# The second layer's first weights made by spaced steps in the last first-layer entry; last carried output evicted before the late work

## Chip, cores and metric

The kernel runs on one core of a Trainium2 chip. The metric is the device time of one execution in microseconds (us), median of three runs; lower is better. A profiled execution gives, beside its own time, a trace of every instruction on the engines: PE (matrix engine, with its weight loads PEld), DVE (vector), ACT (scalar), POOL (GpSimd), and SP, which here only issues DMAs.

## The reference, cut to what matters

Windowed attention over four sequences of 768 tokens gives `x` with 3072 rows of 512; two feed-forward layers follow, and only they are touched by the change:

```python
def _moe_ref(x, w_in, w_out):                 # first layer, d_ff = 2048
    h = x @ w_in
    g = h * (1.0 / (1.0 + np.exp(-1.702 * h)))
    return (g @ w_out).astype(np.float32)

def _moe2_ref(x, w_gate, w_val, w_out):       # second layer, d_ff = 1536
    g = x @ w_gate
    silu = g * (1.0 / (1.0 + np.exp(-g)))
    val = x @ w_val
    return (silu * val @ w_out).astype(np.float32)
```

The weights of both layers come as 64-bit floats, which the kernel turns into 32-bit ones itself.

## The kernel before

**Tiling.** The 3072 tokens are six blocks of 512. The program is a list `seq` of *entries* (layer, block, first unit, end unit). The first layer has 8 units, worked in twelve entries: for each block a first part (units 0 and 1 of block 0, units 0 to 3 of the others), then for each block the rest. The last of these, entry 11, is block 5, units 4 to 7. The second layer has 12 units in sweeps of four, each sweep over all six blocks; its first entry is number 12, units 0 to 3 of block 0.

**One unit** (`unit`) multiplies a block by a unit's in-weights with seven half-size products (Winograd's scheme; each is six matmuls, because every 32-bit operand is split into a rounded high part and a rest). Between the products stand four `chunk`s of six matmuls (down products of earlier units) and eleven *places* `then(0)` to `then(10)`, at which the work of other engines is put into the program. PE needs at its second product the bank that the add `L647` of the unit before frees, at its third ACT's copy `p` (`L622`), and at its last the add `L641`.

**Order.** PE, ACT, DVE and POOL run strictly in program order, which the code writes out by hand; SP's order is left to the scheduler. So an instruction that waits holds up everything behind it on its engine.

**Making a weight tile.** `take_words` (ACT, `L300`), `shift_words` (DVE, `L309`) and `join_words` (DVE, `L314`) turn raw words into a 32-bit tile; `first_sums` and `second_sums` (`L335` to `L340`) make the four sums that the half-size scheme needs; `split_hi` (ACT, `L255`) rounds to the high part and `split_lo` (POOL, `L258`) makes the rest. A unit of the second layer needs the tiles `a`, `s12`, `s34` and, for each pair of units, one `v`.

**The ring.** In-use weight tiles lie in a ring of `NW` = 25 tiles (`Ring`). `take` gives the next one; `give` frees one, but room grows only as the oldest come free, in order. Units 4 to 7 of the first layer hold 22 of the 25. `give_w` frees a unit's in-weights after its last use and its two out-weights at `chunk(3)` two units later.

**Two planners.** `weight_steps` with `prepare` makes tiles straight into the ring; each step asks for room first. Its words use the two `wf` buffers, its sums run on POOL and are written into the raw tile itself. `conversion` with `convert` makes most of the second layer's weights during entries 6 to 10 in steps of a list `todo`, spaced evenly (`due`), in `c` tiles that are stored to DRAM (`keep`) and loaded again later (`load_next`). There the words alternate between `wf` and `wg`, and the sums run on DVE into one tile `s`. In the kernel before, the first four units of the second layer (`fours[-4:]`) are left out of `conversion`; entry 11 makes them by `later_weights` with `prepare(2)` at each place from 2 to 10.

**Tokens.** In the last two units of entry 11 the next entry's tokens are prepared too: four sums in unit 6 and six rests in unit 7, nearly all on POOL (`L545` to `L554`, `L575`).

**The end.** `downs` queues the second layer's down products of one entry, which are spent in the next. The output of bank `y1` of an entry is *carried*: it stands first in the next queue, and costs nothing there. `evict` (`L882`) adds the partial sum. After the last entry the functions in `late` (`L701`, `L708` to `L710`, the casts `L688`, the rests `L695`) are emitted, and then `spend(1000)` empties the queue.

Of the kernel before, what the change touches and what calls it, by code (L numbers as in the profile page):

```python
# [11 lines left out]
F32R = mybir.dt.float32r  # L12
# [7 lines left out]
P = 128  # L20
# [16 lines left out]
HALF = 2 * P  # L37
# [20 lines left out]
def tile_attention_moe_moe(  # L58
# [184 lines left out]
    rings = [Ring(wpool, NW)]  # L243
    wt, wslot = {}, {}
# [136 lines left out]
            yield from weight_steps(1, u)  # L381
        yield None

    def later_weights():
        nraw[0] += 2 * len(fours) - 8
        for u in range(4):
            yield from weight_steps(2, u)
        yield None

    weights = [all_weights()]  # L390
    need, made = [next(weights[0])], [40 * PLAIN]

    def prepare(n):

        for i in range(n):
            if need[0] is None or max(r.room() for r in rings) < need[0]:
                return i
            need[0] = next(weights[0])
            made[0] += 1
        return n  # L400

    def prepare_unit(unit):
        while unit not in ready:
            if not (prepare(1) if unit[0] == 1 else unit[1] >= 4 and load_next()):
                raise ValueError(f"no room for {unit}")

    pool_of, kept, whole_keys = {}, {}, set()
# [8 lines left out]
    def conversion():  # L416
        todo, i0 = [], 2 * NF1

        def words(i):
            return [  # L420
                lambda: (load_raw(i + RB), take_words(i)),
                lambda: shift_words(i, (pool_of["c"], "wg") if i % 2 else (rpool, "wf")),
                lambda: join_words(i),
            ]

        def four(i, ph, u):
            t = {}

            def hi(k, f, n=512):
                def go():  # L430
                    t[k] = pool_of["c"].tile([P, 2, 512], F32R, tag="c", name="c")
                    split_hi(t[k], f(), 0, n)

                return go

            def lo(k, f, n=512):
                def go():
                    split_lo(t[k], f(), 0, n)

                return go  # L440

            def st(k, key, o=0, n=512):
                return lambda: keep(key, t.pop(k)[:, :, :n], o, n)

            def a():
                return bits[i]

            def v():
                return bits[i + 1][:, HALF:]

            def pair(j):
                return lambda: t["s"][:, 2 * j : 2 * j + 2].rearrange("p s n -> p (s n)")

            def sums(f):
                def go():
                    if "s" not in t:
                        t["s"] = pool_of["c"].tile([P, 4, HALF], F32, tag="s", name="s", bufs=1)
                    f(t["s"], bits[i], bits[i + 1], nc.vector)

                return go  # L460

            vkey = (ph, u - u % 2, "v")
            keys = {k: (ph, u, k) for k in ("a", "s12", "s34")}
            half = (u % 2) * HALF
            return [
                sums(first_sums),
                hi("a", a),
                0,
                sums(second_sums),
                lo("a", a),  # L470
                hi("s12", pair(0)),
                1,
                lo("s12", pair(0)),
                st("a", keys["a"]),
                hi("v", v, HALF),
                2,
                lo("v", v, HALF),
                st("s12", keys["s12"]),
                3,
                hi("s34", pair(1)),  # L480
                lo("s34", pair(1)),
                4,
                st("v", vkey, half, HALF),
                5,
                st("s34", keys["s34"]),
            ]

        wide = []
        for j, (ph, u) in enumerate(fours[:-4]):
            i = i0 + 2 * j  # L490
            ws = words(i) + words(i + 1)
            wide.append((ws, four(i, ph, u)))
        todo += wide[0][0]
        for j, (ws, f) in enumerate(wide):
            nxt = wide[j + 1][0] if j + 1 < len(wide) else []
            for x in f:
                todo += nxt[x : x + 1] if isinstance(x, int) else [x]
        return todo

    todo, due = conversion(), [0.0]  # L500

    def convert(left):
        due[0] += len(todo) / max(left, 1)
        while todo and due[0] >= 1.0:
            due[0] -= 1.0
            todo.pop(0)()

    def loads():
        for p0 in range(0, UNITS[2], 4):
# [388 lines left out]
    LAST1 = len(seq)  # L898
# [385 lines left out]
    for n, (ph, b, ua, ub) in enumerate(seq):  # L1284
# [6 lines left out]
        for u in range(ua, ub):  # L1291
            last = u == ub - 1
            upcoming = order[done + 1] if done + 1 < len(order) else None
            if last and ua > 0 and ph == 1:
                base = load_base(ph, b)
            if last and attends and n:
                tok = Tokens(xf.pop(nxt[1]), TE)
            places = PLACES[u - ua] if n > 1 and attends else ()

            def chunk(d):  # L1300
                p = pends[0 if d == 3 else 1]
                if p is not None:
                    p(d)
                elif queue and not (d == 3 and u == ua):
                    share[0] += 84 / 15
                    spend(int(share[0]))
                    share[0] -= int(share[0])

            def after(i):
                follow()  # L1310
                for x in [x for x in defer if x[0] == i]:
                    defer.remove(x)
                    x[1]()
                if i in places:
                    run(steps.pop(0))
                if nxt is not None and (last or ub - u == 2 and not attends):
                    for k in (EARLY if not last else LATE if attends else MAKE).get(i, ()):
                        if k < 0:
                            tok.sum(-1 - k)
                        elif n < NBLK or k:  # L1320
                            tok.split(k)
                        else:
                            tok.split_hi(k)
                            defer.append((i + 1, lambda k=k, x=tok: x.split_lo(k)))
                if i > 1 and n == LAST1 - 1:
                    prepare(2)
                elif i > 1 and need[0] is not None:
                    pace(done * SLOTS + i, last)
                elif i > 1 and todo:
                    convert((seq_slots - 4 - done) * 9 - i + 2)  # L1330
                if n >= LAST1 - 1 and need[0] is None:
                    load_next()
                if i == 9 and upcoming is not None:
                    prepare_unit(upcoming)

            if n == LAST1 - 1 and u == ua:
                while todo:
                    todo.pop(0)()
                weights[0] = later_weights()
                need[0] = next(weights[0])  # L1340
            if ph == 2 and "h" not in pool_of:
                stage_ctx.close()
                raw_ctx.close()
                pool_of["h"] = ctx.enter_context(tc.tile_pool(name="h", bufs=1))
            if n == 1 and u < 3:
                gs = seconds[u]
            elif n:
                gs = unit(ph, u, ops, chunk, after, n < NBLK - 1, ph == 1 and ua > 0, nxt is None and last)
            else:
                gs = firsts[u]  # L1350
            if final[ph, u] == n:
                for k in ("a", "s12", "s34"):
                    give_w((ph, u, k))
                if u % 2 or u + 1 == UNITS[ph]:
                    give_w((ph, u - u % 2, "v"))

            def pend(d, passes=PASSES, ph=ph, b=b, u=u, ua=ua, ub=ub, gs=gs, n=n, base=base):
                down(ph, b, u, u == ua, u == ub - 1, gs, base, dest(ph, ub == UNITS[ph]), d, 0.5 if ph == 1 and not ua else 1.0, passes)
                if final[ph, u] == n and d == 3:
                    for o in range(OUTS[ph]):  # L1360
                        give_w((ph, u, o))

            pends = [pends[1], pend if ph == 1 else None]
            if u == ua and nxt is not None and not attends:
                src = {1: xd, 2: yd}[nxt[0]][nxt[1]]
                tok = load_tokens(src, LATER_TE if n >= NBLK else TE)
            done += 1
# [6 lines left out]
        if n == NBLK - 2:  # L1374
            attn_ctx.close()
            pool_of["c"] = stage_ctx.enter_context(tc.tile_pool(name="cv", bufs=NC))
    for i in sorted(late):
        for f in late[i]:
            f()
# [43 lines left out]
```

## Time and profile before

| | us |
|---|---|
| median of three runs | 1215.75 |
| lowest, highest | 1214.41, 1216.39 |
| the profiled execution, its own time | 1213.07 |
| span of the profiled execution | 1211.3 |
| PE busy in the span | 1150.7 (95%) |
| DVE, ACT, POOL busy | 792.9, 657.3, 637.0 |

The span runs from the first to the last instruction; 1.8 us of the execution lie around it. Times in the trace count from the span's start. A row of the timeline has start, duration, engine, line, operation, output<-input, shape and, in brackets, how long the engine was idle before it and what ended that. Rows of one group are merged where an engine repeats an operation (x6).

### The profile page before, as it was taken

The page shows a single profiled execution, that of the slowest core. Times are in us where ns is not written, and L with a number is a line of the kernel's source. Part 1 is how long each engine was busy: PE and PEld are TensorE (multiplying, and loading weights), DVE is VectorE, ACT ScalarE, POOL GpSimd, SP SyncE. Part 2 cuts the span into 40 slices and gives each one's busy share as a digit, 9 for nine tenths or more (in the row PEclk, how much of TensorE's full clock was granted, in tenths as well). Part 3 has the DMA queues.
Part 4 walks back from the last instruction along what each step waited for, and adds up shares of the span by engine and source line. Part 5 has one row for each costly group of instructions (what it writes and reads, how often), then busy time and mean ns, then how long its engine had stood idle before and what let it go on. Part 6 is the DMA issues. An engine that isn't in the chain of part 4 may idle for free.

```text
span 1211.3 us, 24802 instructions
## 1 busy us (share of the span) xinstructions
PE 1150.7 (95%) x9556; PEld 1067.4 (88%) x9556; DVE 792.9 (65%) x1370; ACT 657.3 (54%) x1419; POOL 637.0 (53%) x518
## 2 busy tenths in 40 slices
PE   4889999999999999989978999999999999999997
PEld 3678888888888888878867999999999999999997
DVE  5886756555657778686645666666666666666665
ACT  4766555555565565555544555555555555555552
POOL 4565230202356685575685655555666565565540
PEclk9899999999999999999989999999999999999999
DMA  9977445352264777869644122166533367333322
GB/s 297 293 250 224 132 131 146 100 157 77 82 188 129 270 262 268 301 214 342 229 146 157 36 70 71 70 226 192 192 106 105 106 244 244 122 106 106 105 71 105
DMA packets 89352, 201.90 MB, mean 167 GB/s; under 512 B 8465, under 2 KB 32529, under 8 KB 86161
## 3 DMA queue, kind: packets, MB, share of 16 engines
q1 hardware_dynamic: 89232, 200.31, 50.6%
q8 instruction: 75, 1.23, 0.4%
q14 instruction: 45, 0.36, 0.1%
HBM read 136.84 MB, written 63.44 MB: 165 GB/s over the span
## 4 chain that ended last, share of the span: by engine, by line
PE 76%; DVE 7%; DMA 6%; ACT 4%; issue 3%; POOL 3%; SPq 0%; DVEq 0%; ACTq 0%; POOLq 0%
PE ps_a L589 24%; PE y L864 15%; PE y L779 15%; PE ps_c L589 11%; PE ps_b L589 8%; DMA raw<-in_wr 3%; DMA vm<-in_vg 2%; PE ps_s L201 1%; DVE wf L309 1%; PE ps_o L174 1%; POOL b L575 1%; DVE wf L314 1%; DMA xd<-xf 1%; ACT wh L300 1%; POOL c L258 1%
## 5 line engine op out<-in xcount | busy, mean ns | idle before, releaser
L589 PE MATMUL ps_a<-b,w 128*128 128x256 f32 x2832 | 403.1, 285 | 13.1 <-ACT p L622 6.0
L589 PEld LDWEIGHTS ps_a<-b,w 128*128 128x128 f32 x2832 | 371.2, 191 | 33.5 <-ACT p L622 12.8
L864 PE MATMUL y<-gs,w 128*128 128x512 f32 x1152 | 301.0, 397 | 0.3 <-DVE gs L745 0.2
L864 PEld LDWEIGHTS y<-gs,w 128*128 128x128 f32 x1152 | 205.7, 190 | 36.6 <-DVE gs L745 1.6
L589 PE MATMUL ps_c<-b,w 128*128 128x256 f32 x1224 | 180.2, 283 | 2.5 <-ACT m L635 1.2
L779 PE MATMUL y<-w,h 128*128 128x256 f32 x1080 | 166.5, 287 | 4.0 <-DVE base L882 3.9
L589 PEld LDWEIGHTS ps_c<-b,w 128*128 128x128 f32 x1224 | 163.1, 191 | 6.2 <-DVE gs L745 2.0
L779 PEld LDWEIGHTS y<-w,h 128*128 128x128 f32 x1080 | 145.8, 194 | 5.3 <-DVE base L882 4.1
L589 PE MATMUL ps_b<-b,w 128*128 128x256 f32 x900 | 136.9, 288 | 14.2 <-DVE ps_b L647 12.1
L575 POOL TENSOR_TENSOR b<-xl,b 128x512 fp32r<-128x512 f32 x93 | 124.1, 1344 | 36.1 <-PE y L779 19.5
L589 PEld LDWEIGHTS ps_b<-b,w 128*128 128x128 f32 x900 | 120.4, 193 | 19.6 <-DVE ps_b L647 13.7
L641 DVE TENSOR_TENSOR ps_a<-m,ps_a 128x256 f32<-128x256 f32 x115 | 48.9, 425 | 102.4 <-PE ps_a L589 72.7
L695 POOL TENSOR_TENSOR h<-f,h 128x512 fp32r<-128x512 f32 x36 | 46.8, 1300 | 117.8 <-ACT h L688 117.8
L631 ACT COPY u<-ps_a 128x256 f32<-128x256 f32 x115 | 43.1, 375 | 105.2 <-PE ps_a L589 105.0
L258 POOL TENSOR_TENSOR w<-wf,w 128x512 fp32r<-128x512 f32 (+1 forms) x40 | 45.8, 1146 | 86.0 <-ACT w L255 85.8
L733 ACT ACTIVATE g<-ps_b 128x512 f32<-128x512 f32 x72 | 43.0, 598 | 87.1 <-DVE ps_b L647 87.1
L695 POOL TENSOR_TENSOR gs<-t,gs 128x512 fp32r<-128x512 f32 x36 | 47.1, 1308 | 79.0 <-ACT gs L688 79.0
L575 POOL TENSOR_TENSOR b<-t,b 128x512 fp32r<-128x512 f32 x57 | 81.3, 1426 | 8.8 <-ACT b L571 8.8
L626 DVE TENSOR_TENSOR ps_b<-p,ps_b 128x256 f32<-128x256 f32 x115 | 49.0, 426 | 39.9 <-ACT p L622 28.7
L571 ACT CAST b<-xl 128x512 fp32r<-128x512 f32 x120 | 75.1, 626 | 0.1
L779 PE MATMUL y<-w,gs 128*128 128x256 f32 x432 | 65.9, 283 | 0.0
L622 ACT COPY p<-ps_a 128x256 f32<-128x256 f32 x115 | 43.3, 377 | 39.3 <-PE ps_a L589 37.9
(154 smaller groups left out, 1805.9 us busy)
## 6 DMA issues: line engine op xcount, KB each, us to landing
raw<-in_wr SPq DMA_DIRECT2D x37, 512.0 KB, 4.5
xl<-yd SPq DMA_DIRECT2D x18, 1024.0 KB, 5.9
wd_s<-c SPq DMA_DIRECT2D x28, 512.0 KB, 5.8
w<-wd_s SPq DMA_DIRECT2D x28, 512.0 KB, 4.9
raw<-in_wr SPq DMA_DIRECT2D x54, 256.0 KB, 5.5
base<-zp SPq DMA_DIRECT2D x48, 256.0 KB, 3.1
vm<-in_vg SPq DMA_DIRECT2D x22, 512.0 KB, 6.1
kbd<-in_kg SPq DMA_DIRECT2D x32, 256.0 KB, 4.2
```

The source lines that it names most:

```text
L258: nc.gpsimd.tensor_sub(w[:, 1, o : o + n], f, w[:, 0, o : o + n].bitcast(F32))
L571: nc.scalar.copy(self.ops[k][:, 0], self.source(k))
L575: self.engs[k].tensor_sub(x[:, 1], self.source(k), x[:, 0].bitcast(F32))
L589: nc.tensor.matmul(ps, w[:, a, o + kc * P : o + kc * P + P], x[:, c, kc, :], start=(start and kc == 0 and (a, c) == PASSES[0]), stop=(kc = ...
L622: nc.scalar.copy(p1, ca[:, :n])
L626: add(cb[:, :n], p1, cb[:, :n])
L631: nc.scalar.copy(u2, ca[:, :n])
L641: add(ca[:, n:], m, ca[:, :n])
L695: eng.tensor_sub(w[:, 1], f(), w[:, 0].bitcast(F32))
L733: nc.scalar.activation(t, c, AF.Silu)
L779: nc.tensor.matmul(region(k, t), ops[j][k][:, c, t * P : t * P + P], w[:, a, o : o + n], start=first and k not in (3, 4, 5, 6), stop=j == ...
L864: nc.tensor.matmul(y, lhs, rhs, start=(first and o == 0 and (a, c) == PASSES[0]), stop=(ends and o == len(gs) - 1 and (a, c) == passes[-1]),)
```

## The change

`later_weights` goes. `conversion` now covers all 18 units; the last four are *straight*: their tiles are taken from the ring instead of `c`, a step that takes one is a pair `(1, step)` and waits for room, and nothing is stored. `convert` gets a second argument, how many steps at the end of the list to keep back: 80 (`STRAIGHT`) during entries 6 to 10, none in entry 11, over whose places the 80 are spaced. Steps that are blocked for room let `due` grow to at most 3. `load_next` is called from entry 12 on instead of 11. At the very end `spend(0)` runs what costs nothing at the head of the queue (the carried eviction and the fetch of partial sums) before the functions in `late`.

```diff
-    def later_weights():
-        nraw[0] += 2 * len(fours) - 8
-        for u in range(4):
-            yield from weight_steps(2, u)
-        yield None
-
@@ prepare_unit
         while unit not in ready:
-            if not (prepare(1) if unit[0] == 1 else unit[1] >= 4 and load_next()):
+            due[0] = 1.0
+            if not (prepare(1) if unit[0] == 1 else load_next() if unit[1] >= 4 else convert(1000, 0)):
                 raise ValueError(f"no room for {unit}")
@@ conversion
-        def four(i, ph, u):
+        def four(i, ph, u, straight):
             t = {}
 
             def hi(k, f, n=512):
                 def go():
-                    t[k] = pool_of["c"].tile([P, 2, 512], F32R, tag="c", name="c")
+                    key = (ph, u - u % 2 if k == "v" else u, k)
+                    if not straight:
+                        t[k] = pool_of["c"].tile([P, 2, 512], F32R, tag="c", name="c")
+                    else:
+                        if key not in wt:
+                            wt[key], wslot[key] = rings[0].take()
+                        t[k] = wt[key][:, :, u % 2 * HALF :] if k == "v" else wt[key]
                     split_hi(t[k], f(), 0, n)
 
-                return go
+                return (0 if k == "v" and u % 2 else 1, go) if straight else go
...
             def st(k, key, o=0, n=512):
+                if straight:
+                    return lambda: ready.add((ph, u)) if k == "s34" else None
                 return lambda: keep(key, t.pop(k)[:, :, :n], o, n)
...
-        for j, (ph, u) in enumerate(fours[:-4]):
+        for j, (ph, u) in enumerate(fours):
             i = i0 + 2 * j
             ws = words(i) + words(i + 1)
-            wide.append((ws, four(i, ph, u)))
+            wide.append((ws, four(i, ph, u, j >= len(fours) - 4)))
...
-    def convert(left):
-        due[0] += len(todo) / max(left, 1)
-        while todo and due[0] >= 1.0:
+    STRAIGHT = 4 * 20
+
+    def convert(left, keep_back):
+        due[0] += (len(todo) - keep_back) / max(left, 1)
+        while len(todo) > keep_back and due[0] >= 1.0:
+            room, f = todo[0] if isinstance(todo[0], tuple) else (0, todo[0])
+            if room > rings[0].room():
+                due[0] = min(due[0], 3.0)
+                return False
             due[0] -= 1.0
-            todo.pop(0)()
+            todo.pop(0)
+            f()
+        return True
@@ the places of a unit
                 if i > 1 and n == LAST1 - 1:
-                    prepare(2)
+                    convert((seq_slots - done) * 9 - i, 0)
...
-                    convert((seq_slots - 4 - done) * 9 - i + 2)
-                if n >= LAST1 - 1 and need[0] is None:
+                    convert((seq_slots - 4 - done) * 9 - i + 2, STRAIGHT)
+                if n >= LAST1:
                     load_next()
...
             if n == LAST1 - 1 and u == ua:
+                while len(todo) > STRAIGHT:
+                    todo.pop(0)()
+            if ph == 2 and "h" not in pool_of:
                 while todo:
-                    todo.pop(0)()
-                weights[0] = later_weights()
-                need[0] = next(weights[0])
-            if ph == 2 and "h" not in pool_of:
+                    due[0] = 1.0
+                    assert convert(1000, 0)
@@ after the last entry
+    spend(0)
     for i in sorted(late):
         for f in late[i]:
             f()
```

## Rows read from the trace of the kernel before

**Rows 1.** The page: busy time, share of the span and instructions.

```profile
PE 1150.7 (95%) x9556; PEld 1067.4 (88%) x9556; DVE 792.9 (65%) x1370; ACT 657.3 (54%) x1419; POOL 637.0 (53%) x518
```

**Rows 2.** Busy time by stretch, around the last first-layer entry.

```profile
core 0: us, PE busy (x) PEld busy (x) DVE busy (x) ACT busy (x) POOL busy (x), PEclk, DMA share, GB/s
582.50:593.05 10.55, 10.55 (x68) 9.51 (x68) 7.97 (x12) 4.85 (x11) 7.58 (x8) 1.00 0.84 283
593.05:603.90 10.85, 10.85 (x68) 9.49 (x68) 5.62 (x10) 5.83 (x13) 4.85 (x6) 1.00 0.74 249
603.90:620.46 16.56, 11.23 (x73) 9.99 (x71) 8.78 (x10) 6.03 (x13) 13.29 (x12) 0.96 0.22 73
620.46:635.03 14.57, 12.36 (x55) 9.78 (x55) 6.83 (x8) 8.46 (x18) 12.19 (x12) 0.81 0.72 255
635.03:644.65 9.62, 5.62 (x24) 4.33 (x25) 4.01 (x5) 5.36 (x12) 8.91 (x10) 0.82 0.35 120
644.65:651.77 7.12, 7.12 (x43) 6.35 (x43) 3.35 (x6) 3.06 (x5) 1.74 (x2) 1.00 0.78 270
```

**Rows 3.** Timeline, from unit 6 to unit 7.

```profile
615.63 2.48 POOL L258 TENSOR_TENSOR w<-raw,w 128x512 fp32r<-128x512 f32 x2
616.97 1.43 DVE L309 TENSOR_SCALAR wf<-wh 128x512 int32<-128x512 int32 x1 [5.22 <-POOL w L258]
618.43 1.63 DVE L314 SCALAR_TENSOR_TENSOR wf<-raw,wf 128x512 int32<-128x512 int32 x1
...
620.46 1.65 PE L589 MATMUL ps_b<-b,w 128*128 128x256 f32 x6 [5.33 <-DVE ps_b L647]
```

**Rows 4.** Timeline, unit 7's last product to the next unit's third.

```profile
635.03 1.71 PE L589 MATMUL ps_a<-b,w 128*128 128x256 f32 x12 [0.96 <-DVE ps_a L641]
...
639.37 1.38 PE L589 MATMUL ps_b<-b,w 128*128 128x256 f32 x6 [2.63 <-DVE ps_b L647]
...
642.71 0.62 ACT L255 CAST w<-raw 128x512 fp32r<-128x512 f32 x1 [0.94 <-POOL raw L340]
...
644.65 0.98 PE L589 MATMUL ps_a<-b,w 128*128 128x256 f32 x6 [1.37 <-ACT p L622]
```

**Rows 5.** Groups by line and shape: busy us, mean ns | idle before.

```profile
L622 ACT COPY p<-ps_a 128x256 f32<-128x256 f32 x115 | 43.3, 377 | 39.3 <-PE ps_a L589 37.9
...
L258 POOL TENSOR_TENSOR w<-raw,w 128x512 fp32r<-128x512 f32 x22 | 28.5, 1310 | 23.7 <-ACT w L255 23.7
...
L255 ACT CAST w<-wf 128x512 fp32r<-128x512 f32 x28 | 17.4, 620 | 12.1 <-DVE wf L314 12.1
...
L335 DVE TENSOR_TENSOR s<-wg 128x256 f32<-128x256 f32 x14 | 14.7, 1052 | 5.7 <-POOL c L258 5.2
...
L340 POOL TENSOR_TENSOR raw<-wf,raw 128x256 f32<-128x256 f32 x11 | 9.5, 861 | 0.0
L258 POOL TENSOR_TENSOR w<-wf,w 128x256 fp32r<-128x256 f32 x12 | 9.5, 789 | 7.8 <-ACT w L255 7.8
```

**Rows 6.** Timeline: a DVE sum alone, and one beside POOL.

```profile
504.32 0.41 DVE L335 TENSOR_TENSOR s<-wg 128x256 f32<-128x256 f32 x1
...
533.32 1.29 POOL L575 TENSOR_TENSOR b<-xl,b 128x512 fp32r<-128x512 f32 x1
533.39 1.49 DVE L335 TENSOR_TENSOR s<-wg 128x256 f32<-128x256 f32 x1 [1.20 <-POOL c L258]
...
534.56 1.46 POOL L575 TENSOR_TENSOR b<-t,b 128x512 fp32r<-128x512 f32 x1
```

**Rows 7.** Timeline: the end.

```profile
1190.67 0.68 DVE L701 TENSOR_TENSOR f<-g,ps_a 128x512 f32<-128x512 f32 x1
...
1194.60 0.68 DVE L882 SCALAR_TENSOR_TENSOR base<-y,base 128x512 f32<-128x512 f32 x1
...
1195.33 6.79 PE L779 MATMUL y<-w,h 128*128 128x256 f32 x42 [3.91 <-DVE base L882]
```

**Rows 8.** Busy time by stretch, the end.

```profile
1195.33:1199.10 3.77, 3.77 (x20) 3.77 (x21) 0.00 (x0) 0.85 (x3) 0.00 (x0) 0.60 0.44 162
```

## The prediction

> **What bounds the kernel now.** I read the page first: the matrix engine (PE) is busy 95% of the span [rows 1], so only stretches in which PE loses time can be won or lost. The busy time by stretch came next, cut at unit borders of the last first-layer entry (block 5, units 4 to 7) [rows 2]. The reader is to see that units 4 and 5 run without a gap (10.55 us of PE in 10.55 us; that is a unit's own length), and that the next three rows have gaps and a granted clock of 0.96, 0.81 and 0.82. At full clock unit 6 would start at about 603.9, unit 7 at 614.4, the first second-layer unit (call it Z) at 625.0, and Z's third product would stand 2.8 us later, at 627.8. It starts at 644.65 [rows 4]. So **16.85 us** are lost here, and what follows runs at full clock with no gap.
>
> Then the timeline, for what ended each wait. POOL runs late; DVE's shift into a `wf` buffer waits 5.22 us for POOL to let the buffer go, and the add that PE needs stands behind it in DVE's queue, so PE waits 5.33 us [rows 3]: 5.3 us lost. By the last product of unit 7 (635.03, nominal 624.3) 10.7 us are lost, and by Z's third product 16.85: first PE waits for a DVE add behind shifts, then for ACT's copy `p`, which is queued behind a cast that waited for sums made on POOL [rows 4]. The second place is the end: PE sits 3.91 us until DVE has evicted one carried bank [rows 7], and then runs at 0.60 of the clock, the lower level of 1.2 GHz for most of that stretch [rows 8].
>
> **The change, part by part.**
>
> *Ring room (who may start when).* The ring has 25 tiles, and units 4 to 7 hold 22 of them (five each, and one `v` for each pair). They come free in order only. Counting `give_w` by hand: three tiles are free in unit 4, one more in unit 5, eight in all at unit 6's third place (`chunk(3)` gives back unit 4's out-weights), more in unit 7. The new weights need 14. So neither kernel can make more than four before unit 6; ten of the 14 fall into units 6 and 7 in both, and "evenly over one entry" isn't reached: the spaced steps stand blocked from the third step place of unit 5 on and then run at up to three a place. Units 4 and 5: I cost the change there at 0. It adds six left-over steps of the unit before and moves 8 sums to DVE; DVE is busy 7.97 of 10.55 us in unit 4 [rows 2], each add that PE needs has about 3 us between its product and its use, and the evenly spaced steps put at most two or three DVE operations before one. If that cover is gone it costs up to 1.5 us.
>
> *Sums leave POOL.* Before, units 6 and 7 give POOL 9 full rests at 1.31, 3 half ones at 0.79, 12 sums at 0.86 [rows 5], and the 10 whole-width operations on the next tokens at about 1.3 [rows 6]: 11.8 + 2.4 + 10.3 + 13.0 = 37.5 us in 21.1 us of PE. POOL is busy 8.91 of the 9.62 us up to Z's third product [rows 2], so it works off a backlog. After, the 12 sums are DVE's: 27.2 us on POOL, still more than 21.1, but the backlog shrinks by 10.3.
>
> *The same sums on DVE.* Alone such a sum takes 0.41 us; beside a running POOL operation it takes 1.49, because it ends only some 0.28 us after that operation, and the next POOL operation is stretched from 1.29 to 1.46 [rows 6]. The mean over this kernel's DVE sums is 1.05 [rows 5]. So 12 sums cost DVE between 5 and 18 us. I take the contended price wherever POOL has work ready and the lone one where it waits for ACT.
>
> *The one `s` tile.* The spaced steps keep all sums in one buffer: the first sum of a unit waits on DVE until POOL has read the unit before it (rest of `s34`). Behind that wait stand the add `L647` and so PE, ACT's curve and casts. This is the wait that takes the place of the `wf` wait; the `wf` wait goes, since the words now alternate between `wf` and `wg`, two buffers each.
>
> *Walking the queues.* In unit 6 DVE has, in order: two sums, a shift and a join, a token rest, `L641`, shift and join, two sums, `L647`. POOL alternates: rest, token sum, rest, token sum, half rest, token sum, the rest of `s34` (ends about 616.4 when each pair takes 1.46 and each join 1.63 [rows 3, 6]), token sum, rest. The two sums that need `s` free end at 618.0 and 619.4, `L647` at 619.85. PE's second product of unit 7 so starts at **619.9** in place of 620.46: 0.6 us won. ACT then has a cast of sums (its two sums on DVE are alone, 0.41 each), two casts, a curve and the copy `p` at 0.62 and 0.38 each [rows 5]: unit 7's third product at 623.4. In unit 7 POOL has two token rests, the rest of `s34`, two token rests, and a rest. DVE's shift, join and four sums go one by one behind them: 626.8, 628.5, 630.0, 631.4, 632.9 and, POOL then waiting for ACT, 633.3; `L641` 633.7. So the last product of unit 7 is at **633.7** in place of 635.03. From here no step of the weights waits for POOL: ACT has three casts and a half one, then curve, cast, cast, curve and the copy `p`, 4.9 us at the prices of [rows 5], and Z's third product starts at **638.3** in place of 644.65. Middle: **-6.3 us**. Drops of the clock in these stretches cost nothing of their own, as PE waits for the copies at the end of each.
>
> How DVE and POOL interleave is the largest unknown. The Trainium skill (SBUF — State Buffer, Who interferes with whom) has a DVE instruction with two SBUF inputs and a reading GpSimd instruction shut each other out for the whole instruction, which speaks against these sums. The pair would then take 1.29 + 0.41 = 1.70 us; the trace shows 1.46 [rows 6], so the exclusion is seen but not in full. By the whole lock the middle would win 3.3 us, a rival below.
>
> *Fewer loads in the last entry.* Reloading starts one entry later; before, there was one place with a free tile. These weights are not read before the first pairs of the second layer, tens of microseconds later: 0.
>
> *The end.* `spend(0)` puts the eviction of the carried bank ahead of the last unit's late functions. Before, it ran at 1194.60, behind DVE's chain that begins at 1190.67 [rows 7]. Its products end at about 1190.8, so it can run there, and the twelve products of PE end at 1191.4; the next 18 products (first and second group) follow without a wait. The third group must wait until ACT has copied the second group's parts, and ACT has three casts ahead of four copies of 0.38: the chain on DVE is 0.9 us later (the eviction of 0.68 [rows 7] and its wait), so that copy ends at about 1195.3. Before, these 18 products ran from 1195.33 to 1199.2. So the third group starts 3.9 us sooner: **-3.9 us**. If the copies come sooner it is the gap and the slow clock, 3.91 + (1 - 0.60) × 3.77 = 5.4; if the later chain holds up the second group, 2.
>
> *Sum.* -6.3 - 3.9 = **-10.2 us**. From the profiled execution's 1213.07 that is 1202.9; that execution is 2.7 us below the median of the runs, so the median goes from 1215.75 to **1205.6**.
>
> **The rivals.**
> - *The lock is whole*, as the page named above has it (12 pairs, each 0.25 us longer, on DVE's path): the middle wins 3.3, the end 3.9, **1208.6**. For it: joins beside POOL take 1.63 [rows 3]. Against it: 1.46 for a pair.
> - *The spacing removes the first stall too.* If POOL reaches the rest of `s34` before DVE asks for `s`, the 4.7 us at 619.9 shrink to under 1 and unit 7 begins without backlog: the middle wins about 11, the end 4 to 5, **1200**. For it: POOL's list is 10 us shorter; against: four token operations stand before that rest in POOL's queue.
> - *DVE becomes the bound.* All 12 sums contended at 1.49 is 18 us more on DVE; that eats the middle's gain whole and leaves the end: **1211.9**.
> - *The end gives nothing*, since the late chain behind the eviction sets the second group: **1209.5**.
> - *Slower.* The one `s` tile, twice: if POOL comes to the rest of `s34` only after all four token sums in unit 6 (4 × 1.3) and all six token rests in unit 7 (6 × 1.3), DVE waits 5.2 and 7.8 us longer than I walked, 13 us in all: **1218.6**. It decides from about 10 us of added waits of the sums for POOL on. Against it: program order puts that rest after three of the four and after two of the six.
>
> **How the numbers follow.** Forecast 0.42, whole lock 0.13, stall gone 0.20, DVE bound 0.11, no end 0.06, slower 0.08. Below 1198.5 I leave 0.05, above 1212.5 the slower case and half of the DVE case: the range is 1198.5 to 1212.5. A measurement of this kernel can tell about 0.2% (2.4 us) from no change; by that faster is 0.84 (all but the slower case and most of the DVE case), same 0.08, slower 0.08.
>
> **What would show it.** In the profile after: DVE's sum `L335` waiting for POOL's `L258` before unit 7, and PE's second product there still 3 to 5 us late; no wait of ACT's casts for POOL sums, and Z's third product some 6 us sooner than 644.65; units 4 and 5 at 10.6 us each; at the end a gap of 1 to 2 us in place of 3.91, ended by ACT's copy, with the clock near 1. The forecast is wrong if units 4 or 5 stretch, if the `s` wait exceeds 5 us, or if the clock falls after a shorter gap at the end.

## The result, and the profile after

The median went from 1215.75 to **1204.58 us**; the ratio is 0.9909 with a 95% interval of 0.9887 to 0.9932, so 8.3 to 13.7 us were won. The profiled execution took 1205.27 us, its span 1203.5. In the tables and texts below *Z* is the first unit of the second layer, as in the prediction, and line numbers after the change are some 11 higher than before.

The page, busy time, share of the span and instructions; it answers to [rows 1]:

```profile
PE 1148.9 (95%) x9556; PEld 1066.6 (89%) x9556; DVE 807.0 (67%) x1386; ACT 656.4 (55%) x1419; POOL 629.2 (52%) x502
```

Sixteen instructions went from POOL to DVE (518 to 502, 1370 to 1386): the sums. PE does the same work (1148.9 us in place of 1150.7), so most of the gain is in the gaps. Behind the opening the two traces run at the same pace to within half a microsecond, except in two places. The first is around the last first-layer entry; busy time by stretch, cut at the x12 row in which each unit begins (columns as in [rows 2]), of before:

```profile
581.59:602.97 21.38, 21.38 (x133) 18.98 (x132) 13.17 (x20) 11.09 (x25) 13.34 (x14) 1.00 0.76 251
602.97:613.53 10.56, 10.56 (x67) 9.53 (x66) 5.79 (x7) 5.32 (x11) 7.30 (x7) 1.00 0.31 115
613.53:635.03 21.50, 13.96 (x68) 11.17 (x66) 10.23 (x11) 9.66 (x20) 18.18 (x18) 0.84 0.55 189
635.03:651.77 16.74, 12.73 (x67) 10.68 (x67) 7.35 (x10) 8.42 (x16) 10.65 (x11) 0.90 0.53 184
```

and of after:

```profile
583.85:606.76 22.91, 21.92 (x133) 18.83 (x132) 18.37 (x29) 11.84 (x26) 11.62 (x10) 1.00 0.87 284
606.76:617.32 10.56, 10.56 (x67) 9.53 (x66) 8.79 (x10) 7.37 (x15) 7.47 (x6) 1.00 0.19 64
617.32:637.57 20.25, 13.56 (x67) 11.65 (x65) 18.48 (x20) 9.40 (x20) 18.41 (x14) 0.83 0.52 178
637.57:648.24 10.67, 10.67 (x66) 9.64 (x67) 4.34 (x8) 5.76 (x11) 3.96 (x4) 1.00 0.74 246
```

The rows are units 4 and 5, unit 6, unit 7, and Z. Units 4 and 5 became 1.5 us longer, unit 7 1.3 us shorter, and Z 6.1 us shorter, as PE has no gap in it any more and POOL is busy 3.96 us there in place of 10.65. In all 70.18 became 64.39 us: **5.8 us** here. What is left of the stall in unit 7 shows in the timeline of after, which answers to [rows 3] and [rows 4]:

```profile
618.27 1.45 POOL L258 TENSOR_TENSOR w<-s,w 128x512 fp32r<-128x512 f32 x1
618.63 1.64 DVE L314 SCALAR_TENSOR_TENSOR wg<-raw,wg 128x512 int32<-128x512 int32 x1
...
620.38 1.30 DVE L335 TENSOR_TENSOR s<-wg 128x256 f32<-128x256 f32 x1
621.36 1.44 POOL L258 TENSOR_TENSOR w<-wf,w 128x512 fp32r<-128x512 f32 x1
621.71 1.37 DVE L336 TENSOR_TENSOR s<-s,wf 128x256 f32<-128x256 f32 x1
623.00 0.42 DVE L658 TENSOR_TENSOR ps_b<-u,ps_c 128x256 f32<-128x256 f32 x1
...
623.47 1.65 PE L600 MATMUL ps_b<-b,w 128*128 128x256 f32 x6 [4.55 <-DVE ps_b L658]
...
637.57 1.70 PE L600 MATMUL ps_a<-b,w 128*128 128x256 f32 x12 [2.15 <-DVE ps_a L652]
...
641.22 0.88 PE L600 MATMUL ps_a<-b,w 128*128 128x256 f32 x6
```

DVE stands in no wait before these rows: from 609.18 on it has no gap of more than about 0.1 us. It is late with its own list, and the add that PE needs (`L658`, before `L647`) comes at the end of it. The list is long because most of it runs beside POOL: the two sums take 1.30 and 1.37 us here, and 0.41 alone [rows 6].

The second place is the end. Its timeline of after answers to [rows 7]; the stretch below it answers to [rows 8]:

```profile
1185.45 2.57 DVE L893 SCALAR_TENSOR_TENSOR base<-y,base 128x512 f32<-128x512 f32 x4
...
1186.53 3.96 PE L790 MATMUL y<-w,h 128*128 128x256 f32 x29
...
1187.93 0.68 DVE L712 TENSOR_TENSOR f<-g,ps_a 128x512 f32<-128x512 f32 x1
...
1191.43 3.13 PE L790 MATMUL y<-w,h 128*128 128x256 f32 x24 [0.94 <-ACT d L812]
```

```profile
1191.43:1197.42 5.99, 5.99 (x48) 5.90 (x49) 2.61 (x7) 0.97 (x3) 0.23 (x1) 1.00 0.32 109
```

All four evictions run in a row, PE goes on without the gap of 3.91, and the gap that is left, 0.94, ends with ACT's copy. The clock stays at 1.00 where it was 0.60. From the last unit's last x12 row (1182.04 before, 1178.62 after) to PE's last matmul (1206.99 and 1199.43) it is 24.95 and 20.81 us: **4.1 us** here.

5.8 and 4.1 are 9.9 us. The two spans differ by only 7.8, because the profiled execution of after was already 1.8 us later at 107 us, in the opening, which the change doesn't touch, and a few tenths more were lost elsewhere.

### The profile page after: what moved, and what is told of

It is laid out like the page before. It is cut to its first block, busy times and chain, and to the rows that moved or that the text cites. A ratio compares the mean times of both kernels' runs of the same rounds, so it can differ in the third digit from the quotient of the medians.

```text
span 1203.5 us, 24803 instructions
## 1 busy us (share of the span) xinstructions
PE 1148.9 (95%) x9556; PEld 1066.6 (89%) x9556; DVE 807.0 (67%) x1386; ACT 656.4 (55%) x1419; POOL 629.2 (52%) x502
## 4 chain that ended last, share of the span: by engine, by line
PE 74%; DVE 10%; DMA 6%; ACT 4%; issue 4%; POOL 1%; SPq 0%; DVEq 0%; ACTq 0%; POOLq 0%
PE ps_a L600 24%; PE y L790 15%; PE y L875 14%; PE ps_c L600 10%; PE ps_b L600 8%; DMA raw<-in_wr 1%; PE ps_s L201 1%; DMA xd<-xf 1%; DVE s L335 1%; DVE wf L309 1%; PE ps_o L174 1%; DMA yd<-base 1%; ACT gs L752 1%; DMA q<-in_qg 1%; DMA w<-in_kg 1%
## 5 line engine op out<-in xcount | busy, mean ns | idle before, releaser
L600 PE MATMUL ps_b<-b,w 128*128 128x256 f32 x900 | 137.1, 289 | 11.2 <-DVE ps_b L658 8.7
L790 PE MATMUL y<-w,gs 128*128 128x256 f32 x432 | 65.9, 283 | 0.0
```

The lines of the kernel that those rows point to most:

```text
L600: nc.tensor.matmul(ps, w[:, a, o + kc * P : o + kc * P + P], x[:, c, kc, :], start=(start and kc == 0 and (a, c) == PASSES[0]), stop=(kc = ...
L790: nc.tensor.matmul(region(k, t), ops[j][k][:, c, t * P : t * P + P], w[:, a, o : o + n], start=first and k not in (3, 4, 5, 6), stop=j == ...
```

## The experiments

Each was timed beside the kernel before; ratios are to that. The last column but one holds the four stretches above (units 4 and 5, unit 6, unit 7, Z), from the x12 rows of each trace. A stretch is that of one execution, which need not be a typical one: the traced execution of e4 is the fastest of its four (1200.82 us), and those of e9 and e11 are the slowest of their ten (1215.38 and 1218.31). Differences of one or two microseconds between sums say little.

| kernel | median us | ratio (95% interval) | stretches, us | sum |
|---|---|---|---|---|
| before | 1215.75; beside the experiments 1213.91 to 1214.74 | 1 | 21.4, 10.6, 21.5, 16.7 | 70.2 |
| after | 1204.58 | 0.9909 (0.9887 to 0.9932) | 22.9, 10.6, 20.3, 10.7 | 64.4 |
| e1_end_only | 1210.02 | 0.9969 (0.9953 to 0.9984) | 21.4, 10.6, 21.5, 16.7 | 70.2 |
| e2_steps_only | 1209.08 | 0.9960 (0.9946 to 0.9973) | 22.9, 10.6, 20.2, 12.2 | 65.9 |
| e3_sums_on_dve | 1211.90 | 0.9980 (0.9968 to 0.9993) | 23.4, 11.9, 17.2, 15.6 | 68.2 |
| e4_spaced_pool_sums | 1202.64 | 0.9910 (0.9888 to 0.9933) | 21.6, 10.6, 16.8, 13.6 | 62.5 |
| e5_token_sums_early | 1201.43 | 0.9901 (0.9886 to 0.9916) | 23.4, 10.7, 16.7, 12.8 | 63.4 |
| e6_one_wf | 1204.91 | 0.9925 (0.9909 to 0.9941) | 22.9, 10.6, 20.3, 12.2 | 66.0 |
| e7_steps_wg | 1214.09 | 0.9999 (0.9987 to 1.0012) | 21.4, 10.6, 21.5, 16.7 | 70.2 |
| e8_pool_sums_early | 1199.05 | 0.9881 (0.9864 to 0.9897) | 21.6, 10.6, 10.6, 17.3 | 60.0 |
| e9_take_early | 1214.03 | 0.9984 (0.9966 to 1.0002) | 21.4, 10.6, 17.9, 20.5 | 70.3 |
| e10_words_last | 1204.06 | 0.9905 (0.9874 to 0.9936) | 22.5, 10.6, 20.8, 12.2 | 66.0 |
| e11_three_a_place | 1215.32 | 1.0006 (0.9993 to 1.0018) | 21.4, 10.6, 25.4, 15.5 | 72.9 |
| e12_later_end | 1202.18 | 0.9906 (0.9891 to 0.9921) | 22.3, 10.6, 13.9, 16.7 | 63.5 |

**The end alone.** Before, plus one line:

```diff
+    spend(0)
     for i in sorted(late):
```

> The kernel before with spend(0) ahead of the late functions and nothing else. Theory (the two parts are independent, and the end is worth what the two traces show between the last unit's last two products and PE's last matmul, 4.1 us): about 1211.6 us, 4 us below the kernel before; at the end a gap of about 1 us that ends with ACT's copy d, the third group some 4 us earlier. Rival (the end only follows from a different state of the queues that the spaced steps leave behind): no gap closes, 1215.7 us.

Measured 0.9969, 3.8 us (1.9 to 5.7) by the median of the kernel before that was timed beside it. The timeline of PE shows the gap of after, with the middle as in before:

```profile
1189.88 3.96 PE L779 MATMUL y<-w,h 128*128 128x256 f32 x29
1194.80 3.13 PE L779 MATMUL y<-w,h 128*128 128x256 f32 x24 [0.95 <-ACT d L801]
```

The rival falls: one line gives the whole of the end.

**The steps alone.** After, less that line:

```diff
-    spend(0)
     for i in sorted(late):
```

> The changed kernel without spend(0): the spaced steps alone. Theory: the trace of after gains 5.5 us from unit 4's start to the third product of the first second-layer unit (7.2 us from unit 6 on, less 1.7 us lost in units 4 and 5), so about 1210 us, with the gap of 3.9 us at the end back. Rival (the medians differ by 11.2 us, and the part that the two traces don't place, about 1.5 us, belongs to the steps): 1208.5 us or less.

Measured 0.9960, 4.9 us (3.3 to 6.6); the interval holds the times of both the theory and the rival. The gap of 3.90 at the end is back:

```profile
1191.74 6.78 PE L790 MATMUL y<-w,h 128*128 128x256 f32 x42 [3.90 <-DVE base L893]
```

The two parts alone make 8.7 us; both together were 8.3 to 13.7. They add within the intervals. Z takes 12.18 here and 10.67 in after, with PE without a gap in both: the granted clock of that stretch is 0.86 here and 1.00 there. So some 1.5 us of Z differ between executions of the same steps.

**Sums on DVE, nothing else.** Before, in `weight_steps`:

```diff
-        first_sums(s, a, b)
+        eng = nc.gpsimd if ph == 1 else nc.vector
+        first_sums(s, a, b, eng)
...
-        second_sums(s, a, b)
+        second_sums(s, a, b, eng)
```

> The kernel before, in which the second layer's sums that its last first-layer entry makes run on DVE in place of POOL; steps, their places, their buffers (sums in the raw tile, words in wf alone) and the end stay. Theory A (what helps is that POOL's backlog shrinks by the sums, 10 us): most of the 7 us comes, 1210 to 1212 us, and ACT's casts of sums no longer wait for POOL. Theory B (what helps is the spacing and the second pair of word buffers, wg): nothing or a loss, 1215 to 1219 us, since DVE still waits for POOL's rest at the wf buffers and now has the sums in its own queue too.

Measured 0.9980, 2.4 us: between the two, about half of what the steps win. The time lies in theory A's range only because the kernel before took 1214.25 us beside it; the gain is not most of 7 us. Unit 7 and Z win 5.4 us, and units 4 to 6 lose 3.4 (35.3 in place of 31.9). The reason that theory B gives falls too: with one pair of `wf` buffers and the old order, no shift waits longer than 1.8 us here, and the one that stands in [rows 3] hardly waits at all:

```profile
618.54 1.05 DVE L309 TENSOR_SCALAR wf<-wh 128x512 int32<-128x512 int32 x1 [0.39 <-issue]
```

**Spaced steps, sums on POOL.** After, in `sums`:

```diff
-                    f(t["s"], bits[i], bits[i + 1], nc.vector)
+                    f(t["s"], bits[i], bits[i + 1], nc.gpsimd if straight else nc.vector)
```

> The changed kernel, but the straight units' sums run on POOL in place of DVE; spacing, wg and spend(0) stay. Theory A (the sums' place is what counts): the backlog on POOL is back, the middle wins next to nothing, 1211 to 1213 us, the end's 4 us alone. Theory B (spacing and word buffers count): 1204 to 1207 us, like the changed kernel, perhaps with units 4 and 5 at 10.6 us again.

Measured 0.9910, the same as after. Theory A falls: with the sums back on POOL nothing is lost. Units 4 and 5 take 21.6 in place of 22.9 us, so 1.3 of the 1.5 us that after loses there are the price of sums on DVE. Busy time of unit 7 and Z, and what PE waits for in unit 7:

```profile
612.97:629.74 16.77, 12.61 (x67) 10.86 (x66) 9.20 (x11) 7.49 (x16) 16.68 (x15) 0.90 0.47 155
629.74:643.30 13.56, 10.83 (x67) 9.46 (x66) 4.05 (x7) 7.46 (x14) 10.27 (x10) 1.00 0.55 192
```

```profile
618.86 0.62 ACT L255 CAST w<-s 128x512 fp32r<-128x512 f32 x1 [3.59 <-POOL s L336]
...
621.09 1.28 PE L600 MATMUL ps_a<-b,w 128*128 128x256 f32 x6 [4.01 <-ACT p L633]
```

DVE is busy 9.20 us in unit 7 in place of 18.48, and POOL carries its load into Z (10.27), but now PE has only one long wait in each unit, for a copy that ACT makes late because a cast waits for POOL's sums. The stall changed its engine more than its size.

**One pair of word buffers.** After, straight units through `wf` alone:

```diff
-(pool_of["c"], "wg") if i % 2 else (rpool, "wf")
+(pool_of["c"], "wg") if i % 2 and i < i0 + 2 * (len(fours) - 4) else (rpool, "wf")
```

> The changed kernel, but the words of the straight units all go through the two wf buffers, as in the kernel before; order, spacing, the s tile and the end stay. Theory C (the second pair of word buffers is what helps, as it ends the waits of 5.2 and 5.1 us of DVE's shift for POOL's rests): the shifts wait again and 4 to 5 us of the middle are lost, 1208 to 1210 us. Theory D (the order and spacing of the steps help: the next unit's words are made ahead, between the rests of the unit before, and the last tiles are ready sooner): 1204 to 1206 us.

**The second pair, given to before.** Before, in `next_weights` for the second layer's odd words:

```diff
-        shift_words(i)
+        shift_words(i, (pool_of["c"], "wg") if odd else None)
```

> The kernel before, but in the last first-layer entry the second word of each unit goes through the wg buffers; the two steps a place, the sums on POOL in the raw tile and the end stay. Theory C (word buffers): 4 to 6 us faster than the kernel before, 1208 to 1210 us, without the 5.2 us wait of the shift. Theory D (order and spacing): 1213 to 1215 us, as DVE and ACT still meet each unit's words, sums and casts one straight after the other.

Theory C falls in both: e6 has the stretches of e2 to 0.1 us, and e7 is the kernel before. The wait that the prediction put down to the `wf` buffer is still there in e7, 5.24 us, although every second word now goes through `wg`:

```profile
616.08 2.48 POOL L258 TENSOR_TENSOR w<-raw,w 128x512 fp32r<-128x512 f32 x2
616.15 0.62 ACT L255 CAST w<-raw 128x512 fp32r<-128x512 f32 x1 [2.70 <-POOL raw L340]
616.68 0.66 ACT L300 ACTIVATE wh<-raw 128x512 f32<-128x512 f32 x1
617.44 1.41 DVE L309 TENSOR_SCALAR wf<-wh 128x512 int32<-128x512 int32 x1 [5.24 <-POOL w L258]
```

The trace names POOL's rest, which ended at about the same time. The shift reads what ACT's `L300` writes, and starts 0.10 us after it; `L300` stood behind a cast, and the cast waited 2.70 us for POOL's last sum. POOL's rest reads `raw` and not `wf`.

**ACT's word taken ahead of the casts.** Before, in `weight_steps`:

```diff
         for i, n in enumerate(("s12", "s34")):
+            if ph == 2 and u < 3 and i == 0:
+                take_words(nraw[0])
             yield 1
```

> The kernel before with one instruction of each unit moved: ACT takes the next unit's first raw word before the casts of this unit's sums, no longer behind them. Sums on POOL, two steps a place, buffers and the end stay. Theory E (the 5.2 us wait of DVE's shift was for ACT's taken word, and that stood behind a cast that waits for POOL's sums; the order on ACT is what the spaced steps mend): the waits of 5.2 us go, PE's wait of 5.33 us shrinks to 3 us or less, and 2 to 5 us of the middle's gain come, 1209 to 1212 us. Rival F (POOL's backlog sets the time wherever ACT's word stands): 1213 to 1215 us.

PE's wait fell to 2.88 us, as theory E had it. The shift's waits fell by two microseconds, to 3.26 and 3.12, and didn't go: now they end with POOL's sum that reads the words in `wf` (`L340` here, `L339` in before).

```profile
615.60 0.72 POOL L340 TENSOR_TENSOR raw<-wf 128x256 f32<-128x256 f32 x1
...
616.35 0.93 DVE L309 TENSOR_SCALAR wf<-wh 128x512 int32<-128x512 int32 x1 [3.26 <-POOL raw L340]
```

The time is the same within its interval (0.9966 to 1.0002), as rival F expected. Unit 7 won 3.6 us and Z lost 3.7, with a new wait for ACT's copy behind casts of the last unit's sums:

```profile
619.35 0.98 PE L592 MATMUL ps_b<-b,w 128*128 128x256 f32 x6 [2.88 <-DVE ps_b L650]
...
643.77 1.65 PE L592 MATMUL ps_a<-b,w 128*128 128x256 f32 x6 [5.14 <-ACT p L625]
```

After that wait PE's rows are slow: from this product to Z's end it is 9.4 us at a granted clock of 0.73, in before 7.1 at 1.00 (the last line of [rows 2]).

```profile
643.77:653.19 9.42, 9.42 (x42) 8.39 (x43) 3.35 (x6) 3.06 (x5) 1.72 (x2) 0.73 0.41 156
```

Up to this product e9 had been 2.2 us ahead of before, counted from unit 4 (60.8 to 63.1); the slow clock took it back.

**Words behind the tiles.** After, in the straight units:

```diff
+            if j >= len(fours) - 4:
+                todo += [x for x in f if not isinstance(x, int)] + nxt
+                continue
             for x in f:
```

> The changed kernel, but among the straight units the next unit's six word steps stand behind the unit's own tiles, as in the kernel before, in place of between them; spacing, sums on DVE, wf and wg, the s tile and the end stay. Theory E (order): 2 to 5 us are lost, 1206 to 1210 us. Rival G (the even spacing over the places is what helps, in whatever order): 1203 to 1205 us, like the changed kernel.

Measured 0.9905, like after. Theory E falls as the explanation of the whole: the order of the words among the tiles is not what the steps win by.

**An earlier end of the steps, in before; a later one, in after.**

```diff
-                    prepare(2)
+                    prepare(3 if last else 2)
```

> The kernel before with three steps a place in place of two in the last unit (unit 7) of its last first-layer entry, so that the last tile is made at place 6, no longer at place 9; order, buffers, sums on POOL and the end stay. Theory H (what the change wins is won in the first second-layer unit, since its last steps stand earlier in the program and are out of the way by then): that unit's stretch falls from 16.7 us to 12 us or less, unit 7 keeps its stalls or grows by up to 2 us, in all 3 to 5 us won, 1210 to 1212 us. Rival I (POOL's load decides, as the sums are still POOL's): what the one unit wins the other loses, 1213 to 1215 us.

```diff
-                    convert((seq_slots - done) * 9 - i, 0)
+                    convert((seq_slots - done) * 9 - i + 4, 0)
```

> The changed kernel with the spaced steps stretched to end four places later: the last unit's three tiles are then begun at places 8 to 10 of unit 7, and five steps run right before the first second-layer unit. Order, sums on DVE, buffers and spend(0) stay. Theory H: the first second-layer unit is late again by 3 to 6 us, 1207 to 1210 us. Rival I (DVE having the sums is enough, wherever the steps end): 1203 to 1206 us, like the changed kernel.

Unit 7 and Z of e11, then of e12:

```profile
615.04:640.45 25.41, 15.49 (x68) 12.68 (x66) 12.61 (x14) 10.85 (x22) 20.18 (x20) 0.80 0.45 162
640.45:655.96 15.51, 12.47 (x67) 10.81 (x67) 4.33 (x8) 7.20 (x14) 8.18 (x9) 0.89 0.56 202
```

```profile
614.42:628.34 13.92, 11.09 (x68) 9.50 (x67) 13.30 (x16) 8.46 (x18) 12.12 (x9) 1.00 0.67 226
628.34:644.99 16.65, 12.56 (x68) 10.77 (x66) 6.95 (x12) 7.34 (x14) 9.84 (x9) 0.90 0.59 201
```

Theory H falls on both sides: in e11 Z takes 15.5 us and not 12, and in e12 Z is late again by 6.0 us but unit 7 wins 6.3. Where the steps end decides in *which* unit PE waits (e12: 13.9 and 16.7, after: 20.3 and 10.7), and hardly how long in all (30.6 and 30.9). So the gain of 6.1 us in Z, which looks like the heart of the matter in the trace of after, depends on where the steps end; most of it can stand in unit 7 as well.

**Less work in units 6 and 7.** After, the token sums and the first split one unit earlier, alone (e5) and with e4's edit (e8):

```diff
-                if nxt is not None and (last or ub - u == 2 and not attends):
+                if nxt is not None and (last or ub - u == (3 if n == LAST1 - 1 else 2) and not attends):
```

> The changed kernel, but the four token sums and the first token split of the last first-layer entry stand in unit 5, where the weight steps are blocked for room, in place of unit 6. Theory (the work that POOL and DVE share in units 6 and 7 sets the stall that is left; four POOL operations of 1.3 us leave it): the wait of 4.55 us before unit 7's second product shrinks to 0 to 2 us, 1200 to 1202 us. Rival (DVE's queue is late by its own operations, whatever POOL does): 1204 us, the wait stays over 3.5 us.

> The changed kernel with the straight units' sums on POOL and the token sums and first token split one unit earlier, both edits together. Theory (both take load from units 6 and 7 at different engines, so they add): 1198 to 1201 us, below the changed kernel by 4 us or more. Rival (with the sums back on POOL, ACT's casts wait for them whatever the tokens do): 1202 to 1204 us.

In e5 the wait before unit 7's second product falls from 4.55 to 0.99 us, but a new one of 4.03 stands at unit 7's last product:

```profile
617.74 0.98 PE L600 MATMUL ps_b<-b,w 128*128 128x256 f32 x6 [0.99 <-DVE ps_b L658]
...
631.81 2.93 PE L600 MATMUL ps_a<-b,w 128*128 128x256 f32 x12 [4.03 <-DVE ps_a L652]
```

So the rival falls: what POOL does beside it largely sets how late DVE's list is (of the work that moved, only a token rest of 0.89 us was DVE's own). The four stretches are 63.4 in place of after's 64.4 and e2's 65.9, 1 to 2.5 us better, and the median lies within the expected range. e8 has the lowest time of all, 1199.05 us, ratio 0.9881 (0.9864 to 0.9897), against 0.9909 (0.9887 to 0.9932) for after: its four stretches are 60.0 us, 4.4 below after. The two intervals just overlap, but the stretches agree with the medians. Unit 7 and Z of e8, and the wait that is left:

```profile
613.42:623.98 10.56, 10.56 (x67) 9.53 (x66) 6.60 (x9) 6.99 (x16) 10.48 (x11) 1.00 0.71 247
623.98:641.27 17.29, 12.83 (x67) 11.23 (x66) 4.05 (x7) 7.46 (x14) 11.93 (x12) 0.80 0.56 197
```

```profile
626.57 0.62 ACT L255 CAST w<-s 128x512 fp32r<-128x512 f32 x1 [5.32 <-POOL s L336]
...
632.14 1.65 PE L600 MATMUL ps_a<-b,w 128*128 128x256 f32 x6 [4.46 <-ACT p L633]
```

Unit 7 runs without a gap, and all that is still lost from unit 6 on, 6.7 us, stands in Z: one wait for ACT's copy, behind a cast that waits for POOL's sums, and a granted clock of 0.80.

## Why the prediction was right, and where it was not

*The sum.* 10.2 us were forecast; 11.2 came by the medians, 9.9 by the two places of the traces. Beside the experiments the kernel before had medians of 1213.91 to 1214.74, by which after's 1204.58 would be 9.3 to 10.2 us, so 9.9 is the better figure. The forecast case happened in its outline: a stall left in unit 7, Z early, the end's gap closed but for 0.94. Parts of the path to it were wrong, and in the middle two errors nearly cancel (+0.9 and -1.5 us, below): there the closeness of the number is in part luck.

*The end* (forecast 3.9). Right in size and in mechanism: 4.1 in the trace, 3.8 alone in e1. The step that had the third group wait for ACT's copy is the row that ends the last gap, and the clock stayed up.

*The queues of the middle* (forecast 6.3). By its own steps: unit 7's second product, counted from unit 6's x12 row, was to come 0.6 us sooner and came 0.8 sooner (16.71 and 17.49); unit 7's last product 1.3 sooner, and came 1.3 sooner (30.81 and 32.06); Z's third product 6.3 sooner, and came 7.2 sooner (34.46 and 41.68). The 0.9 is a wait for ACT's copy `p` that the forecast kept in Z (4.6 us from unit 7's last product to Z's third; it is 3.65, without a gap). The prices behind this held: sums beside POOL took 1.30 to 1.52, joins 1.64 to 1.67, POOL's rests beside a sum 1.44 to 1.48. The count of sums didn't: the prediction has eight in units 4 and 5 and twelve in units 6 and 7, of sixteen in all; six and ten ran there, and the ten took 12.1 us of DVE, inside the 5 to 18 that it allowed for twelve.

*Units 4 and 5* (forecast 0, at most 1.5). Mis-sized: 1.5. The prediction itself named stretched units 4 or 5 as a sign that it is wrong, and this sign came. The cover that was named was not enough: two of the six sums there ran beside POOL, at 1.33 and 1.51 us, and the add behind the second came late for unit 4's last product.

```profile
593.73 1.51 DVE L340 TENSOR_TENSOR s<-wf,s 128x256 f32<-128x256 f32 x1
...
595.63 1.70 PE L600 MATMUL ps_a<-b,w 128*128 128x256 f32 x12 [0.56 <-DVE ps_a L652]
```

The rest are two waits of 0.2 us for ACT's copies and PE rows that are slower behind the waits. e4, with the sums on POOL, takes 21.6. This is why the middle as a whole was 5.8 and not 7.2.

*The wait read in [rows 3]*. Wrong about what came last, and half right about the cause. Two things ended before the shift began at 616.97, in before:

```profile
614.26 0.73 POOL L339 TENSOR_TENSOR raw<-wf 128x256 f32<-128x256 f32 x1
...
616.23 0.66 ACT L300 ACTIVATE wh<-raw 128x512 f32<-128x512 f32 x1
```

The last was ACT's word, at 616.89; POOL's sum, which reads the words in `wf`, had ended 2.0 us earlier. e7 takes only the buffer out of the way and the wait stays; e9 takes only ACT's word out of the way and the wait falls by 2.0 us, to the end of that sum. With the sums on DVE (e3) both are gone. So POOL's sums lay behind the wait, along two paths, and no run took both paths away while the sums stayed on POOL in the old order. The prediction took the engine that the trace names as the last releaser at its word, though ACT's word and POOL's rest ended at about the same time and the rest doesn't read the buffer.

*"Sums leave POOL"* as the source of the gain. Not needed: e4 keeps all of the gain with the sums on POOL. Alone (e3) the move is worth 2.4 us, half of the 4.9. So the forecast walked the right queue for this kernel, but the walk doesn't show which edit earns what.

*The `s` tile*. The wait foreseen there didn't come up: POOL had read the tile at 619.72 and DVE came to its sum at 620.38. The stall of 4.55 is DVE's own list at the prices it pays beside POOL. The walk gave the right time because the two paths end within 0.7 us of each other; that is luck.

*The rivals.* "The end gives nothing" and the slower case fall with the result. "The spacing removes the first stall too" falls as well: 4.55 us of the stall stay, behind DVE's list and not behind `s`; e5 and e8, with less work in units 6 and 7, remove that stall and move the wait on. "DVE becomes the bound" is half right: DVE is busy 18.48 of 20.25 us in unit 7, and it bounds that unit, yet the middle still won. "The lock is whole" falls on its price: POOL's rests beside a sum take 1.44 to 1.48 and not 1.70.

*What stays open.* Four edits took one part of the spaced steps away (sums on DVE, `wg`, order of words, place of the end), and none lost more than 2 us; four gave one part to before, and only the sums gained. What all spaced kernels share and all others lack is that the next unit's words and first sums, which need no room in the ring, are made while unit 5 waits for room. From unit 6's x12 row on, the traces of before and its variants all have five shifts and twelve sums; those of after and its variants have four shifts and ten sums (e4 eight). Before asks for room before the second word. That this head start is the common cause is argued from these counts; no run took it away by itself. The spaced kernels share other things that no run took away by itself either: the sums lie in the `s` tile and not in the raw tile, up to three steps run at one place, and nothing is reloaded in entry 11.

## What to carry to other kernels

When several in-order engines pass work to each other and the stretch has more of it than time, taking one wait away can move it to the next engine or the next unit, as in e4, e5, e9, e11 and e12: judge by the whole stretch (here four units), not by the row that shrinks. Making first what needs no scarce room may be what helped here; that isn't shown. An eviction that frees an accumulator belongs ahead of the last unit's private chain: here one line gave 4 us.

## What the runs showed of the hardware

A DVE sum of two SBUF operands costs more than three times its lone time beside POOL, and POOL pays less: the sum is 0.41 alone and 1.30 to 1.52 beside POOL in after, and POOL's own 1.29 becomes 1.44 to 1.48. A join is 0.68 alone and 1.64 to 1.67 beside POOL, and a whole-width POOL operation behind it takes 1.71 to 1.75. The Trainium skill (SBUF — State Buffer, Who interferes with whom) says that a DVE instruction with two SBUF inputs and a reading GpSimd instruction contend; the rows agree, but not with a lock that holds for the whole of both instructions, which would add 0.41 to POOL's beside a sum and not the 0.15 to 0.19 measured.

The clock can eat what a mended wait wins. In e9 PE waited 5.14 us once, and the stretch from there to Z's end took 9.4 us at a granted clock of 0.73, in place of 7.1 at 1.00; in before a gap of 3.91 us at the end was followed by a stretch at 0.60 [rows 8]; behind the gap of 0.94 in after it was 1.00.
